# Batch 0's q and k loaded as f32 rows of all heads, turned on TensorE as f32, and a new order of the first steps

## The chip, the cores and the metric

The kernel runs on one core of a Trainium2 chip. The metric is the device time of one execution in microseconds (us); lower is better. TensorE (PE in the profile) multiplies matrices into PSUM; VectorE (DVE), ScalarE (ACT) and GpSimd (POOL) work on tiles; SyncE (SP) only issues transfers. Transfers are also issued by GpSimd, which alone can cast f32 to bf16 on the way, and by ScalarE. All of them run on the same 16 DMA engines.

## The reference

```
q, k, v: (8, 8, 576, 64) f32        # batch, heads, tokens, head dim
scores = q @ k^T / 8, kept where 0 <= row - col < 64, else -1e9
attn   = softmax(scores) @ v
x      = attn as (4608 tokens, 512)  # heads side by side
h      = x @ w_in                    # (4608, 2048)
out    = (h * cos(h)) @ w_out        # (4608, 512) f32
```

## The kernel before

**Tiling.** Attention runs by batch, by head pair p (4 pairs, two heads on 128 partitions) and by unit j (64 query rows that see 128 keys at most). A group is up to four units, one PSUM bank of scores. The feed-forward part runs by token tiles of 512 (mt 0 to 8); mt 0 is tokens 0 to 511 of batch 0 and is computed in two halves of 256 tokens. From mt 1 on, feed-forward matmuls (`first`, line 453, into `h_ps`; line 609, into `out_ps`) are laid out by a loop, and the attention steps of the next batch are put between them by a plan with times (`at`, `pump`). That part is the same in both kernels.

**The first stretch** is written out by hand: the string `FIRST` is a list of steps, each issued in that order; an engine runs its own instructions in that order. A step is a name and its arguments; the last letter is often the engine (a ScalarE, d VectorE, p GpSimd, s SyncE). The names:

- `Lq0.p`, `Lk0.p` load q, k of batch 0, one head pair: pair 0 as f32 on SyncE (`load_plain`, then `cq`, `ck` cast it), pairs 1 to 3 through GpSimd with a cast (`load_heads`), 128 runs of 2304 bytes. `Lq1`, `Lk1` are batch 1, `Lq2`, `Lk2` batch 2, `Lv0.c`, `Lv1.c` chunks of v (128 tokens by 8 heads, 1024 runs of 256 bytes), `Lwi.i`, `Lwo.i` quarters of w_in and w_out (512 runs of 2 KB each).
- `tq`, `tk` turn q, k of a pair of batch 0 on TensorE (18 transposes of 64x64 bf16 into a PSUM tile of the pool `ps_t`, which has three), `pq`, `pk` copy them out to `qT` (scaled) and `kT`. `Tq`, `Tk`, `Pq`, `Pk` do so for batch 1.
- For a group: `s` scores (line 293 puts the mask, line 309 adds the products), `m` the row maximum (line 319, VectorE), `e` the exponentials (line 336, ScalarE, four instructions), `i` the reciprocal of the sums (line 346), `n` the product with it (line 353, mostly GpSimd), `w` the turn of the weights (line 364), `c` their copy out to `wT`. `G...` are the same steps for groups of batch 1 and the last rows of batch 0.
- `z...`, `y...` copy v into the odd slots that lie across chunks; `v.a.g` is the product with v for two pairs and a half (line 403), `x.a.g` its copy to `xT`. `h.g.f` is the feed-forward product of half g and block f (line 417; needs both `x.0.g` and `x.1.g`), `S` its sine, `g` the gate; `o`, `oc` the second product (line 436) and its copy out. `io`, `mk`, `mc` make the masks, `ms` clears blocks for later batches.

Groups of batch 0 are, before, four units in a row of one pair: `s.p.g` is pair p, units 4g to 4g+3. `FILL` adds transposes and a matmul without use at two groups.

Of the kernel before, what the change touches and what calls it, by code (L numbers as in the profile page):

```python
# [10 lines left out]
def _safe_warn(msg, *a, **kw):  # L11
# [14 lines left out]
GF = 4  # L26
# [18 lines left out]
FILL = (6, 12)  # L45
# [5 lines left out]
    "io ms.0.d Lq0.0 Lk0.0 ms.1.d mk cq.d ms.2.d mc ck.a tq.0 Lq0.1 pq.0.d Lk0.1 tk.0 pk.0.a s.0.0.0 "  # L51
    "Lq0.2 tq.1 tk.1 m.0.0 pq.1.a ms.3.d s.0.1.1 Lk0.2 tq.2 pk.1.d s.1.0.2 Lq0.3 Lk0.3 tk.2 s.1.1.3 "
    "e.0.0 tq.3 m.0.1 Lq1.0 Lk1.0 Lq1.1 pq.2.d pk.2.d Lk1.1 tk.3 m.1.0 s.2.0.4 Lv0.0 Lv0.1 Tq.0 Lv0.2 "
    "pk.3.d m.2.0 e.0.1 pq.3.a i.0.0 e.1.0 Tk.0 s.3.0.0 Tq.1 e.2.0 Lv0.3 Lwi.0 Pq.0.d i.1.0 Lwi.1 m.3.0 "
    "m.1.1 i.2.0 Pk.0.a e.3.0 Lwi.2 Tk.1 n.1.0.p s.2.1.1 Pq.1.d Gs.10.2 m.2.1 Gs.9.4 n.0.0.p Pk.1.a "
    "n.2.0.p i.3.0 e.1.1 w.0.0 zA.0.d w.1.0 c.0.0.d Gs.12.0 w.2.0 n.3.0.p i.0.1 c.1.0.d zA.1.d c.2.0.d "
    "e.2.1 zB.0.s zB.1.s n.0.1.p i.1.1 w.3.0 v.0.0 c.3.0.d x.0.0.a s.3.1.3 Gm.10 v.1.0 m.3.1 i.2.1 "
    "Gs.11.2 Gm.9 Gm.12 n.1.1.p x.1.0.a e.3.1 ms.4.d w.0.1 w.1.1 c.1.1.a i.3.1 h.0.0.1 h.0.1.4 tb "
    "n.2.1.p c.0.1.d Lwi.3 w.2.1 h.0.2.0 n.3.1.p v.0.1 S.0.0 Gm.11 w.3.1 S.0.1 h.0.3.3 Lwo.0 S.0.2 "
    "c.2.1.d c.3.1.d v.1.1 zC.s g.0.0 S.0.3 h.0.4.2 ms.5.d x.0.1.a x.1.1.d h.0.5.1 g.0.1 h.1.0.4 g.0.2 "  # L60
    "g.0.3 S.0.4 ms.6.d h.0.6.0 h.1.1.3 S.0.5 S.1.0 Lq1.2 S.0.6 g.0.4 S.1.1 g.1.0 h.1.2.2 Lk1.2 ms.7.d "
    "Lq1.3 h.0.7.4 g.0.5 h.1.3.1 Lv1.0 Lwo.1 g.1.1 S.1.2 h.1.4.3 g.0.6 Lk1.3 S.0.7 h.1.5.0 g.1.2 h.1.6.2 "
    "Lwo.2 g.0.7 S.1.3 S.1.4 S.1.5 Lwo.3 h.1.7.4 Lv1.1 S.1.6 g.1.3 g.1.4 S.1.7 g.1.5 Lv1.2 g.1.6 tb2 "
    "Tk.2 Lv1.3 Pk.2.d Ge.10 Tq.2 Pq.2.d Tq.3 Ge.9 Ge.12 o.0.0.1 Pq.3.d Tk.3 o.1.0 Pk.3.d Lv0.4 Lq2.0 "
    "Ge.11 Gs.14.3 Gi.10 Gm.14 g.1.7 Lq2.1 Gs.13.0 Lq2.2 o.0.1.2 Gi.9 o.2.0 Ge.14 Gn.10.p Gm.13 Gc.10 "
    "Gi.12 Gs.8.3 o.1.1 Gs.16.4 Gm.8 o.3.0 Ge.13 o.2.1 Gs.15.0 Gi.11 oc.0.d Gn.9.p o.3.1 Gn.12.p o.0.2.3 "
    "Gi.14 Gm.15 Gs.17.1 oc.1.d Gc.9 Gn.11.p Gi.13 Gm.16 o.1.2 Ge.8 Ge.16 Ge.15 y.1.d Gn.14.p yA.p Gi.8 "
    "Gc.12 Gm.17 o.0.3.0 Gi.16 Gn.13.p yB.p Gc.11 Gn.8.p Lq2.3 Lq2.4 Lq2.5 o.2.2 Gn.16.d Gw.8 Gc.14 "
    "Gc.13 Lk2.0 Gp.8.d o.3.2 Gi.15 Gw.16 Lk2.1 Ge.17 Lk2.2 o.1.3 Gn.15.d V.0 Gp.16.d oc.2.a Gw.15 Gi.17 "
    "Lk2.3 o.2.3 V.1 Gp.15.d X.0.a Gn.17.d X.1.d V.2 V.3 X.2.a X.3.d Gc.17 o.3.3 oc.3.a Gs.18.4 Gm.18 "  # L70
    "Ge.18 Lk2.4 Gi.18 Gn.18.d Gc.18 Lk2.5 Lv1.4 "
# [4 lines left out]
def kernel(  # L76
# [28 lines left out]
    first_q = moe.tile([128, 2, d_model], F32, tag="out", name="qT", bufs=OUTS).rearrange("p a f -> p (a f)").bitcast(BF16)  # L105
    qtiles = [first_q[:, S * i:S * i + S] for i in range(PAIRS - 1)]
    qtiles.append(const.tile([128, S], BF16, name="qT3"))
    turned = const.tile([128, PAIRS, S], BF16, name="qT")
    qtiles += [turned[:, p] for p in range(PAIRS)]
    qsets = [const.tile([128, PAIRS, NU, 2, 64], BF16, name=f"qB{i}") for i in range(2)]  # L110
    qblocks = [qset[:, p] for qset in qsets for p in range(PAIRS)]
    vtiles = [const.tile([128, NU - 1, d_model], BF16, name=f"v{i}") for i in range(2)]
    w_in_sb = const.tile([128, PAIRS, d_ff], BF16, name="w_in")
    w_out_sb = const.tile([128, n_ff, d_model], BF16, name="w_out")
    w_in_v = moe_w_in.rearrange("(a p) f -> p a f", p=128)
    w_out_v = moe_w_out.rearrange("(a p) f -> p a f", p=128)
    ident = const.tile([128, 128], BF16, name="ident")
    mask = const.tile([128, 3, 128], F32, name="mask")
    mask16 = const.tile([128, 6, 128], BF16, name="mask16")
# [16 lines left out]
    def copy(engine, out, in_):  # L136
        {"a": nc.scalar.copy, "p": nc.gpsimd.tensor_copy}.get(engine, nc.vector.tensor_copy)(out, in_)  # L137
# [15 lines left out]
    def cast_masks():  # L153
        for lo, hi, of in ((0, 3, 0), (3, 5, 1), (5, 6, 1)):
            nc.scalar.copy(mask16[:, lo:hi], mask[:, of:of + hi - lo])


    def rows_tile(name):
        return ld.tile([128, NC * H * D], BF16, tag=name, name=name)

    def load_heads(name, b, p0=0, n=PAIRS):
        if (name, b) not in st:
            st[name, b] = rows_tile(name)[:, 0:PAIRS * RC * D].rearrange("p (a x) -> p a x", a=PAIRS)
        src = {"q": q, "k": k}[name][b, 2 * p0:2 * p0 + 2 * n]
        nc.gpsimd.dma_start(out=st[name, b][:, p0:p0 + n],
                            in_=src.rearrange("(a h) (p c) d -> (h p) a (c d)", h=2, c=RC))

    def load_plain(name):
        rows = moe.tile([128, 2, d_model], F32, tag="out", name="rows", bufs=OUTS).rearrange("p a f -> p (a f)")[:, 0:RC * D]
        st["rows", name] = rows  # L170
        nc.sync.dma_start(out=rows, in_={"q": q, "k": k}[name][0, 0:2].rearrange("h (p c) d -> (h p) (c d)", c=RC))

    def cast_plain(name, engine):
        if (name, 0) not in st:
            st[name, 0] = rows_tile(name)[:, 0:PAIRS * RC * D].rearrange("p (a x) -> p a x", a=PAIRS)
        copy(engine, st[name, 0][:, 0], st.pop(("rows", name)))
# [49 lines left out]
    def tr_q(b, p):  # L226
        st["tq", b, p] = transposed("q", b, p)

    def put_q(b, p, engine=None):
        of, to = in_order(st.pop(("tq", b, p)), qtiles[b * PAIRS + p], b)  # L230
        if b:
            copy(engine, to, of)
        elif engine == "a":
            nc.scalar.mul(to, of, scale)
        else:
            nc.vector.tensor_scalar(to, of, scale, None, ALU.mult)
# [31 lines left out]
    groups = [[(0, p, j) for j in range(GF * g, GF * g + GF)] for p in range(PAIRS) for g in range(TU // GF)]  # L268
# [13 lines left out]
    def g_scores(n, which):  # L282
        s_ps = bank((BANKS if n < n_listed else S_BANKS)[which], "s_ps")
        units = groups[n]
        if n == FILL[1]:
            nc.tensor.matmul(out=s_ps, lhsT=ident, rhs=mask16[:, 0:4].rearrange("p u c -> p (u c)"), start=True, stop=True,
                             skip_group_check=True)
        s_ps = s_ps[:, 0:len(units) * 128].rearrange("p (u c) -> p u c", c=128)
        if n < n_first:
            m0 = 2 if units[0][2] else 0  # L290
            for h in range(2):
                d = slice(64 * h, 64 * h + 64)
                nc.tensor.matmul(out=s_ps[d].rearrange("p u c -> p (u c)"), lhsT=ident[d, d],
                                 rhs=mask16[d, m0:m0 + len(units)].rearrange("p u c -> p (u c)"),
                                 start=True, stop=False, skip_group_check=True)
# [61 lines left out]
    def g_trans(n):  # L357
        w, u = st.pop(("w", n)), len(groups[n])
        if n in direct:
            st["tw", n] = t_ps = ps_t.tile([128, GF, 128], BF16, tag="t", name="tw_ps")  # L360
            for i in range(GF if n == FILL[0] else 0):
                nc.tensor.transpose(t_ps[:, i], ident, ident)
            for i in range(u):
                nc.tensor.transpose(t_ps[:, i], w[:, i], ident)  # L364
            return
        wT = att.tile([128, GF, 128], BF16, tag="wT", name="wT", bufs=20)
        nc.sync.dma_start(out=wT[:, 0:u], in_=w[:, 0:u].rearrange("p u c -> p (u c)"), transpose=True)
        st.update({("wT", unit): wT[:, i] for i, unit in enumerate(groups[n])})
# [172 lines left out]
    make_identity(nc, ident)  # L541
# [6 lines left out]
    def spread_first(lo, hi):  # L548
        return lambda i, engine: spread_v(0, i, engine, lo, hi)

    steps = {"Lq0": lambda p: load_heads("q", 0, p, 1) if p else load_plain("q"),
             "Lk0": lambda p: load_heads("k", 0, p, 1) if p else load_plain("k"),
             "cq": lambda engine: cast_plain("q", engine), "ck": lambda engine: cast_plain("k", engine),
             "Lq1": lambda p: load_heads("q", 1, p, 1), "Lk1": lambda p: load_heads("k", 1, p, 1),
# [4 lines left out]
             "tq": lambda p: tr_q(0, p), "tk": lambda p: tr_k(0, p), "Tq": lambda p: tr_q(1, p), "Tk": lambda p: tr_k(1, p),  # L559
             "pq": lambda p, engine: put_q(0, p, engine), "pk": lambda p, engine: put_k(0, p, engine),  # L560
# [4 lines left out]
             "s": lambda p, g, which: g_scores(2 * p + g, which), "m": lambda p, g: g_max(2 * p + g),  # L565
             "e": lambda p, g: g_exp(2 * p + g), "i": lambda p, g: g_inv(2 * p + g),
             "n": lambda p, g, engine: g_norm(2 * p + g, engine), "w": lambda p, g: g_trans(2 * p + g),
             "c": lambda p, g, engine: g_put(2 * p + g, engine), "v": values_half, "x": put_x_half,
# [80 lines left out]
```

## Time and profile before

| | |
|---|---|
| time, median of 3 runs | 308.87 us (308.71 to 309.77) |
| profiled execution: span from first to last instruction | 306.3 us |
| its own time beside the span | not given by the page; median less span is 2.6 us |
| busy: TensorE, VectorE, ScalarE, GpSimd | 97%, 75%, 76%, 63% |
| granted TensorE clock | 1.00 |
| first `h` matmul (line 417) | 21.18 us |
| first matmul of token tile 1 (line 453) | 57.17 us |
| moved by GpSimd's queue q0 | 100192 packets, 18.06 MB |
| moved by SyncE's queue q1 | 59568 packets, 23.38 MB |

The page follows one execution. Busy time counts overlapping instructions of an engine once, and matmuls are pipelined, so 97% is not the share of the peak. The chain of waits goes back from the last instruction through what released each step. In the tables of queues a packet is one descriptor, that is one run of bytes; the share is the sum of their times against the 16 engines' time and passes 100% where several are in flight on an engine.

### The profile page before, as it was taken

The numbers are of one execution on the slowest core, as the hardware profiler recorded it, in microseconds if no ns is written. First come the engines' busy times: TensorE is split into PE (matmuls) and PEld (weight loads), VectorE is DVE, ScalarE is ACT, GpSimd is POOL, SyncE is SP. The second block draws the span as 40 slices with busy tenths as digits, with TensorE's granted clock in tenths as the row PEclk, the third lists the DMA queues.
The fourth block names the chain that finished last, engine by engine and source line by source line (L and its number), as shares of the span: only waits on it lengthen the run. The fifth ranks groups of instructions, "written<-read, shape, count | busy, mean of one in ns | idle before, by whom it ended". The sixth has DMA issues, their size and how long they took to land.

```text
span 306.3 us, 7904 instructions
## 1 busy us (share of the span) xinstructions
PE 296.2 (97%) x2616; PEld 159.0 (52%) x2616; DVE 228.5 (75%) x908; ACT 234.3 (76%) x785; POOL 192.5 (63%) x228
## 2 busy tenths in 40 slices
PE   3889999999999999999999999999999999999996
PEld 2768844545555555445544555454545554454443
DVE  5999978599769976798579857986698668235801
ACT  5998799677997799779976997699879986116600
POOL 8998579995659669967998599959903930000000
PEclk9999999999999999999999999999999999999999
DMA  7999999999999995999999999999794643011011
GB/s 146 179 212 192 200 180 130 121 149 191 226 113 116 175 223 80 121 133 232 125 121 137 231 143 104 157 221 148 86 137 107 169 78 141 2 68 71 1 67 70
DMA packets 159945, 42.14 MB, mean 138 GB/s; under 512 B 148256, under 2 KB 155168, under 8 KB 159904
## 3 DMA queue, kind: packets, MB, share of 16 engines
q0 software_dynamic: 100192, 18.06, 80.1%
q1 hardware_dynamic: 59568, 23.38, 40.6%
q8 instruction: 20, 0.33, 0.4%
q14 instruction: 21, 0.17, 0.2%
q10 hardware_dynamic: 144, 0.20, 0.2%
HBM read 36.70 MB, written 9.44 MB: 151 GB/s over the span
## 4 chain that ended last, share of the span: by engine, by line
PE 90%; POOL 4%; DMA 2%; DVE 1%; ACT 1%; issue 1%; POOLq 0%; DVEq 0%; ACTq 0%
PE h_ps L453 35%; PE out_ps L609 35%; PE h_ps L417 5%; PE s_ps L303 4%; PE out_ps L436 4%; PE o_ps L384 3%; DMA k<-in_k_dram 2%; POOL w L353 2%; PE tq_ps L219 1%; POOL v L188 1%; PE out_ps L465 1%; PE s_ps L309 1%; PE tw_ps L364 1%; POOL w_in L204 1%; ACT e L336 1%
## 5 line engine op out<-in xcount | busy, mean ns | idle before, releaser
L609 PE MATMUL out_ps<-w_out,gT 128*128 128x512 bf16 x496 | 117.3, 379 | 0.0
L453 PE MATMUL h_ps<-xT,w_in 128*128 128x512 bf16 x512 | 115.3, 379 | 0.3
L595 ACT ACTIVATE sin<-h_ps 128x512 f32<-128x512 f32 x128 | 73.7, 598 | 32.7 <-PE h_ps L453 31.4
L598 DVE TENSOR_TENSOR gT<-h_ps,sin 128x512 bf16<-128x512 f32 x128 | 82.1, 685 | 21.9 <-ACT sin L595 21.2
L336 ACT ACTIVATE e<-s,negm 128x128 f32<-128x128 f32 (+1 forms) x256 | 97.1, 382 | 0.6 <-DVE negm L324 0.6
L353 POOL TENSOR_TENSOR w<-e,rden 128x512 bf16<-128x512 f32 (+1 forms) x74 | 70.0, 962 | 36.6 <-DVE rden L346 18.8
L453 PEld LDWEIGHTS <-w_in 128*128 128x128 bf16 x512 | 48.8, 98 | 54.7 <-issue 0.4
L609 PEld LDWEIGHTS <-gT 128*128 128x128 bf16 x496 | 45.9, 98 | 44.2
L324 DVE CUSTOM_DVE_ANT_0 s<-s_ps,mask 128x128 f32<-128x128 f32 (+1 forms) x256 | 56.4, 279 | 1.7 <-PE s_ps L309 0.9
L336 ACT ACTIVATION_READ_ACCUMULATOR e<-s,negm 128x1 f32 x256 | 48.3, 189 | 0.0
L182 POOL DMA_DIRECT2D q<-in_q_dram x36 | 28.3, 785 | 10.7 <-DMA q<-in_q_dram 4.0
L188 POOL DMA_DIRECT2D v<-in_v_dram x40 | 34.4, 878 | 0.3 <-issue 0.2
L182 POOL DMA_DIRECT2D k<-in_k_dram x36 | 28.2, 783 | 3.9 <-DMA k<-in_k_dram 1.2
L137 ACT COPY out_sb<-out_ps 128x512 f32<-128x512 f32 (+1 forms) x18 | 10.2, 566 | 24.5 <-PE out_ps L609 18.4
L346 DVE RECIPROCAL rden<-den 128x4 f32<-128x4 f32 (+1 forms) x79 | 13.1, 166 | 19.0 <-ACT e L336 18.6
L303 PEld LDWEIGHTS <-qB 128*128 128x128 bf16 x216 | 16.5, 98 | 14.2
L137 DVE CAST xT<-o_ps 128x512 bf16<-128x512 f32 x24 | 15.5, 677 | 10.1 <-PE o_ps L384 10.1
L137 DVE COPY out_sb<-out_ps 128x512 f32<-128x512 f32 x18 | 12.4, 690 | 13.2 <-PE out_ps L609 12.5
L324 DVE DVE_READ_ACCUMULATOR2_ANT negm<- 128x1 f32 x256 | 21.3, 83 | 0.0
L303 PE MATMUL s_ps<-kT,qB 128*128 128x128 bf16 (+1 forms) x216 | 21.2, 216 | 0.0
L137 POOL COPY v<-v 64x1536 bf16<-64x1536 bf16 (+3 forms) x12 | 18.8, 1570 | 0.3
L137 DVE COPY qB<-tq_ps 64x384 bf16<-64x384 bf16 (+1 forms) x40 | 15.6, 390 | 0.4
(70 smaller groups left out, 257.8 us busy)
## 6 DMA issues: line engine op xcount, KB each, us to landing
out_dram<-out_sb SPq DMA_DIRECT2D x16, 512.0 KB, 7.5
v<-in_v_dram POOLq DMA_DIRECT2D x32, 128.0 KB, 5.7
q<-in_q_dram POOLq DMA_DIRECT2D x36, 96.0 KB, 8.6
k<-in_k_dram POOLq DMA_DIRECT2D x36, 96.0 KB, 8.5
w_in<-in_moe_w_in_dram POOLq DMA_DIRECT2D x4, 512.0 KB, 8.7
w_out<-in_moe_w_out_dram POOLq DMA_DIRECT2D x4, 512.0 KB, 10.8
wT<-w SPq DMA_TRANSPOSE x68, 4.4
q<-in_q_dram POOLq DMA_DIRECT2D x7, 144.0 KB, 6.0
```

The costliest lines, as they stand in the source:

```text
L137: {"a": nc.scalar.copy, "p": nc.gpsimd.tensor_copy}.get(engine, nc.vector.tensor_copy)(out, in_)
L182: nc.gpsimd.dma_start(out=st[name, b][:, c].rearrange("p (h d) -> p h d", h=H), in_=src.rearrange("h p d -> p h d"))
L188: nc.gpsimd.dma_start(out=vt.rearrange("p (h d) -> p h d", h=H), in_=v[b, :, c * 128:c * 128 + n, :].rearrange("h p d -> p h d"))
L303: nc.tensor.matmul(out=s_ps[:, u, 0:64 * chunks].rearrange("p (a t) -> p a t", a=chunks), lhsT=qblocks[(b % 2) * PAIRS + p][:, j].rearrang ...
L324: nc.vector.tensor_tensor_reduce(out=s[:, u, c], in0=s_ps[:, u, c], in1=mask[:, 2 - j % 2 if j else 0, c], scale=-scale if b else -1.0, sc ...
L336: nc.scalar.activation(e[:, u, c], s[:, u, c], AF.Exp, bias=negm[:, u:u + 1], scale=1.0 if n < n_first else -1.0, accum_out=den[:, u:u + 1])
L353: (nc.gpsimd if engine == "p" else nc.vector).tensor_tensor(out=w[:, 0:u], in0=e[:, 0:u], op=ALU.mult, in1=rden[:, 0:u].unsqueeze(2).to_br ...
L417: nc.tensor.matmul(out=h_ps[:, half * e:half * e + half], lhsT=w_in_sb[:, ks, ff * 128:ff * 128 + 128], rhs=st["xT", 0][:, ks, half * g:ha ...
L453: nc.tensor.matmul(out=st["h", ff], lhsT=w_in_sb[:, ks, ff * 128:ff * 128 + 128], rhs=st["xT", mt][:, ks], start=start, stop=stop)
L595: nc.scalar.activation(sin, h_ps, AF.Sin, bias=math.pi / 2.0)
L598: nc.vector.tensor_tensor(out=gt[:, e], in0=h_ps, in1=sin, op=ALU.mult)
L609: nc.tensor.matmul(out=o_ps[e], lhsT=gT[ff // 2][:, ff % 2, ms * 128:ms * 128 + 128], rhs=w_out_sb[:, ff], start=ff == 0, stop=ff == n_ff - 1)
```

## The change

Batch 0's q and k are loaded by chunks of 128 tokens and all heads as f32 (`L.q.c`, `L.k.c`; 1024 runs of 256 bytes, the fifth chunk has 64 tokens), on SyncE, one of them on ScalarE. They are staged in the tile of w_out (the fifth chunk in a tile of its own). TensorE turns each chunk as f32, four transposes of 128x128 into one PSUM tile (`t.q.c`, `t.k.c`), and one copy per chunk casts it into place for all four pairs (`p.q.c`, `p.k.c`). Groups of batch 0 are now two pairs by two units, so that one group needs one chunk of q: `s.a.g` is pairs 2a and 2a+1, units 2g and 2g+1. FILL goes, and `FIRST` is a new order. In it GpSimd's queue begins with v and batch 1, and takes w_in by quarters 1, 2, 0, 3. On the engines, the first entries of the new order are:

```
SyncE:  k3 q3 q0 k1 q1 q2 k2, then q4 k4     (each 1024 runs, q4 and k4 512)
ScalarE: table load, k0, masks, p.q.0, e.0.0, p.q.2, e.1.0, e.1.1, e.0.1, Pk.1, e.1.3, e.0.3, e.0.2, x.1.0
GpSimd: ident, v0, iota, k of batch 1 (pairs 0, 1), v1, q of batch 1 (pairs 0, 1), w_in 1, v3, w_in 2,
        clear, w_in 0, n.0.0, v2, n.1.0, z, w_in 3, n.0.1, z, v4 of batch 1, n.1.3, w_out 1, ...
VectorE: masks, p.k.3, p.q.3, p.k.0, m.0.0, p.q.1, p.k.1, m.1.0, i.0.0, m.1.1, m.0.1, p.k.2, i.1.0, Pk.0, c.0.0,
        m.1.3, i.1.1, p.k.4, n.1.1, i.0.1, p.q.4, m.0.3, Pq.0, m.0.2, i.1.3, c.0.1, c.1.0, c.1.1, i.0.3, m.1.2, x.0.0
TensorE: t.k.3 t.q.3 t.q.0 t.k.0 s.0.0 t.q.1 s.1.0 t.k.1 t.q.2 s.1.1 s.0.1 t.k.2 Tk.0 w.0.0 s.1.3 t.k.4 Tk.1 s.0.2
        t.q.4 s.0.3 Tq.0 w.0.1 w.1.0 w.1.1 Gs.8 s.1.2 Gs.10 v.0.0 Gs.9 v.1.0 Tq.1 w.1.3 h.0.2 h.0.3 h.0.5 ...
```

```diff
-    first_q = moe.tile([128, 2, d_model], F32, tag="out", name="qT", bufs=OUTS).rearrange("p a f -> p (a f)").bitcast(BF16)
...
+    stage = w_out_sb.rearrange("p a f -> p (a f)").bitcast(F32).rearrange("p (c x) -> p c x", c=8)
...
+    ident32 = const.tile([128, 128], F32, name="ident32")
...
-    def load_plain(name):
-        rows = moe.tile([128, 2, d_model], F32, tag="out", name="rows", bufs=OUTS).rearrange("p a f -> p (a f)")[:, 0:RC * D]
-        st["rows", name] = rows
-        nc.sync.dma_start(out=rows, in_={"q": q, "k": k}[name][0, 0:2].rearrange("h (p c) d -> (h p) (c d)", c=RC))
...
+    def load_rows(name, c, queue):
+        (nc.scalar if queue == "a" else nc.sync).dma_start(
+            out=rows_of(name, c).rearrange("p (h d) -> p h d", h=H),
+            in_={"q": q, "k": k}[name][0, :, 128 * c:min(128 * c + 128, S)].rearrange("h p d -> p h d"))
+
+    def turn_rows(name, c):
+        of = rows_of(name, c)
+        n = of.shape[0]
+        st["t", name, c] = t_ps = ps_t.tile([128, PAIRS, n], F32, tag="t", name=f"t{name}_ps")
+        for p in range(PAIRS):
+            nc.tensor.transpose(t_ps[:, p], of[:, 128 * p:128 * p + 128], ident32[:n, :n])
+
+    def put_rows(name, c, engine):
+        t_ps = st.pop(("t", name, c))
+        to = (first_q if name == "q" else k_tile(0))[:, :, 128 * c:min(128 * c + 128, S)]
...
-    groups = [[(0, p, j) for j in range(GF * g, GF * g + GF)] for p in range(PAIRS) for g in range(TU // GF)]
+    groups = [[(0, p, j) for p in (p0, p0 + 1) for j in (j0, j0 + 1)] for p0 in (0, 2) for j0 in range(0, TU, 2)]
...
-        if n == FILL[1]:
-            nc.tensor.matmul(out=s_ps, lhsT=ident, rhs=mask16[:, 0:4].rearrange("p u c -> p (u c)"), start=True, stop=True,
-                             skip_group_check=True)
...
-            for i in range(GF if n == FILL[0] else 0):
-                nc.tensor.transpose(t_ps[:, i], ident, ident)
```

## The prediction

> **What bounds the kernel now.** I read four views: the chain of waits, the timeline of TensorE around the first feed-forward matmul, the transfer queues in short windows, the timelines of VectorE and GpSimd up to 22 us. Engines and lines of the chain first:
>
> ```profile
> PE 90%; POOL 4%; DMA 2%; DVE 1%; ACT 1%; issue 1%; POOLq 0%; DVEq 0%; ACTq 0%
> ```
>
> TensorE is 90% of it. The timeline shows from where (start, length, engine, line):
>
> ```profile
> 20.72 0.62 PE L364 MATMUL tw_ps<-ident,w 128*128 128x128 bf16 x8
> 21.18 1.93 PE L417 MATMUL h_ps<-xT,w_in 128*128 128x256 bf16 x16
> ...
> 57.17 2.76 PE L453 MATMUL h_ps<-xT,w_in 128*128 128x512 bf16 x12
> ```
>
> From 21.18, the first `h`, matmuls follow each other almost without a gap, to 57.17 (second token tile) and on to the end. So the time is the start of the first `h`, plus TensorE's work behind it, plus new stalls. Behind 57.17 the program is the same. What lies ahead of 21.18 is attention on batch 0, fed by transfers. The queues (packets, MB, share of 16 engines), in windows 43 to 46 us, 17 to 20 us, 7 to 11 us, 75 to 76 us (the last two lines):
>
> ```profile
> q0 software_dynamic: 3651, 0.46, 240.9%
> ```
> ```profile
> q0 software_dynamic: 608, 0.61, 122.7%
> ```
> ```profile
> q0 software_dynamic: 729, 0.75, 116.5%
> ```
> ```profile
> q1 hardware_dynamic: 154, 0.31, 89.6%
> q0 software_dynamic: 155, 0.02, 28.2%
> ```
>
> q0 is GpSimd's queue, q1 SyncE's. Per engine (divide by 16) a descriptor costs: a 256-byte run of v, 3651 in 3 us, 13 ns; a 2 KB run of w_in, 608 in 3 us, 79 ns; a 2304-byte run of q or k, some 648 (81 of the 729 are under 512 bytes) in 4 us, 99 ns. In the last window q0 has small v runs and q1 large stores: 155 against 154, one for one. A small descriptor that shares with a queue of large ones waits for a large one each time: 104 ns per pair instead of 13.
>
> **The change part by part.** *Loads of batch 0.* Out go two plain loads and six pair loads (128 runs of 2304 bytes each). In come eight loads of 128 rows by 8 heads, 1024 runs of 256 bytes, 64 per engine, and two halves. Seven of the full ones go through SyncE in the order k3 q3 q0 k1 q1 q2 k2, then q4 k4; k0 goes through ScalarE behind its table load (2.24). At the same time GpSimd's queue, which before issued all of q and k first, gets v0, both k pairs of batch 1, v1, both q pairs, w_in 1, v3, w_in 2, w_in 0, none with a wait ahead. Its issues (0.56 to 0.9 each) run ahead of its transfers, so it is never empty.
>
> Per engine: SyncE's data flows from 2.3 (as the plain loads do), GpSimd's from 3.9. By 3.9 SyncE has moved 122 descriptors. Then 70 (rest of q3, q0) + 64 (k0) + 64 (v0), 13 ns each: 2.6, so q0 and k0 land at 6.5. Then one for one: k of batch 1, 16 x (99 + 13) = 1.8, to 8.3; v1, 64 x 26 = 1.7, to 10.0 (k1 done); q of batch 1, to 11.8; w_in 1, 32 x (79 + 13) = 2.95, to 14.7, when SyncE's 128th lands, the end of q1; v3 to 16.4 (q2); w_in 2 to 19.4; w_in 0 to 22.3, SyncE's 256th: k2. If SyncE were not held, k2 would land at 6.5 + 256 x 0.013 = 9.9. I take 22.3, since the window shows that share to a percent; 9.9 and 24 (a slower plain descriptor) bound it.
>
> The Trainium skill, page "DMA: Bandwidth & Descriptors", section "Queues, rings and completion order", says that an engine drains a whole packet, typically 9 to 17 descriptors, from one ring before it turns to the next. By that rule small descriptors would go in bunches and k2 would land near the early bound; the 154 to 155 above speaks against it here.
>
> *Turning.* 144 transposes of 64x64 go (18 took 0.46 once warm, 3.7 in all), 40 of f32 come. None is in the trace; bounds are 0.10 each (four bf16 128x128 ones took 0.40) and four times that. I take 0.7 a chunk, nearer the bf16 row. TensorE waits for data then, so only k2's 0.7 is on the path (0.4 to 1.6).
>
> *From k2 to the first `h`.* TensorE runs in order: t.k.2 stands ahead of s.1.3, s.0.2, s.0.3, s.1.2 and w.0.0, all needed before the first `h`. p.k.2 stands in VectorE's queue ahead of i.1.0, which releases n.1.0, GpSimd's second product. VectorE, per operation start to start from its timeline: max 0.645 (two took 1.29), turned copy 0.65, wT copy 0.39, reciprocal 0.1, x copy 0.65, half copy 0.35, product 0.65. Landed 22.4, t.k.2 to 23.1, p.k.2 to 23.9. Then up to x.0.0: four max 2.6, Pk.0 and Pq.0 1.3, four wT copies 1.55, five reciprocals 0.5, p.k.4 and p.q.4 0.7, n.1.1 0.65, x.0.0 0.65: 7.95, to 31.8. One wait in it, 0.4, for t.q.4, s.0.3: 32.2. GpSimd's chain from i.1.0 at 24.0 is nearly as long: three products at 1.04, two v copies at 1.07, the issues of w_in 3 (0.8) and of batch 1's v 4 (0.7), 6.8 in all, to 30.8, then w.1.3. ScalarE's e.1.3, e.0.3, e.0.2, x.1.0 end at about 31.9. So the first `h` starts at 32.2, 11.0 later than 21.18.
>
> *TensorE's work behind it.* The same 128 `h`, 64 `o`, 72 transposes of batch 1; one group of wT turns (4) and six score matmuls move behind the first `h`: 0.25 + 0.2 = 0.45. FILL's filler (0.4 + 0.4) lay ahead of 21.18 in waiting time: nothing.
>
> *VectorE behind it.* After x.0.0 it owes Gm.8, Gm.9, Gm.10 (12 x 0.21), n.1.2 and Pq.1 (1.3): 3.8, before g.0.2, while TensorE's four `h` and three turns cover 4.2; banks come free a little late: 0.6, from 0 to 1.5.
>
> *Clock.* In the trace 18 transposes take 0.69 up to 9.7 us and 0.46 from 10.3. The Trainium skill, "TensorE: Matmul & The Clock Gate", Part 1, puts such a pair down to a clock that halves after an idle window of about 3.4 us and doubles after a busy one; by it the emptier start would add an estimate of up to 1.7 at the first `h`. I take nothing for it; the upper end holds a cold stretch.
>
> *Hidden edits.* The iota moves behind one v issue (0.9) and the masks with it, to about 5.5; the scores need them at 9. Staging lies in w_out's tile, so w_out's loads wait for the turns; the last, issued near 45, is needed past 55 and landed in 10.8 before: without that cover 1 to 3. The batch-0 casts (0.46, 0.67) go into the first wait.
>
> *Sum.* The page gives no separate time for the profiled execution; its span is 306.3, the median 308.87, and I keep the 2.6 between them. 308.87 + 11.0 + 0.45 + 0.6 = 320.9, say 321.
>
> **The rivals.** *B, the loads are not held.* SyncE's small descriptors go in bunches and k2 lands near 10. Then VectorE decides: q0, k0 at 6.5, t.q.0 and t.k.0 to 8.0, p.k.0 to 8.7, scores and first max to 10.2; behind that p.q.1, p.k.1, three max, a reciprocal and p.k.2, 4.0, then the 7.95 and the 0.4: x.0.0 ends at 22.6, 1.4 late: 308.87 + 1.4 + 0.45 = 310.7, or 313 with the slow turns. For it: both plain loads of the trace landed 2.9 to 3.2 after issue. Against: the one-for-one window. This is also the case that the Trainium skill's rule on packets (above) would make.
>
> *C, faster.* Scores of all heads start as soon as two chunks are there, and ScalarE's exponentials set the pace: seven groups at 1.40 (four of 0.35), p.q.2 0.65, Pk.1 0.67, x.1.0 0.6: 11.7 behind e.0.0. If e.0.0 starts at 7.3, against 8.18 before, the first `h` is at 19.0: 308.87 - 2.2 + 0.45 = 307.1. It decides only if q0 lands by 4.5 and k2 by 9, and if VectorE's list of 13 behind p.k.0 is shorter than its rows say.
>
> *D, no change.* Between B and C: e.0.0 at 9, `h` at 20.7, 308.8.
>
> **How the numbers follow.** About 0.5%, 1.5 us, is what a measurement of this kernel can tell from no change. The forecast has 0.70, with 317 to 325 as its own range (k2 from 18.5 to 24.5, turns, stall). B has 0.19, C 0.07, D 0.04. Slower 0.89, same 0.04, faster 0.07. The range reaches down to 310 to take in B, up to 325; it leaves out C, D and some 0.08 above.
>
> **What would show it.** In the profile after: in the windows from 7 to 20 us, q1 has about as many packets as q0 whenever q0 moves 1 KB packets, and q1 is not through before 20; TensorE's t.k.2 ends past 20; between p.k.2 and x.0.0 VectorE is busy without a break; the first `h` is near 32 and the second tile's first matmul near 69. The forecast is wrong if q1's seven loads have landed by 12, or if the first `h` starts before 24.

## The result, and the profile after

| | before | after |
|---|---|---|
| time, median of 4 runs | 309.32 us | 325.89 us (324.59 to 326.81) |
| ratio | | 1.0523, 95% interval 1.0477 to 1.0569 |
| span of the profiled execution | 306.3 | 323.8 (its time 325.61) |
| first `h` | 21.18 | 37.17 (forecast 32.2) |
| k2 landed | | 27.13 (forecast 22.3) |

The change costs 5.2%. The forecast, 321.0, had the direction and the mechanism; 325.89 lies just above its range (310 to 325). Some executions take over 1.5% longer than the fastest of the same kernel, in a slower state, and medians here and below leave them out (one each of e5, e7 and e8). The chain of waits by engine and by line, from the page:

```profile
PE 80%; DMA 7%; DVE 5%; ACT 4%; SPq 2%; issue 1%
PE h_ps L462 34%; PE out_ps L616 30%; DMA w_out<-in_k_dram 6%; PE s_ps L314 3%; ACT e L347 3%; PE o_ps L393 3%; PE h_ps L426 3%; SPq L176 2%; PE out_ps L445 2%; DMA wT<-w 2%; PE tq_ps L238 1%; DVE w L364 1%; PE out_ps L474 1%; DVE s L335 1%; PE s_ps L320 1%
```

TensorE carried 90% of the chain before. Now 6% of it, 18.85 us, is one transfer: k2, staged in w_out's tile, from its issue at 8.28 to its landing at 27.13; SyncE's issues ahead of it (L176) are on the chain too. TensorE's timeline (start, length, engine, line, what it waited for in brackets):

```profile
11.37 0.53 PE L320 MATMUL s_ps<-kT,qB 64*64 64x64 bf16 x8 [0.22 <-DVE kT L136]
17.86 1.09 PE L185 MATMUL tq_ps<-ident,w_out 128*128 128x128 f32 x4 [5.97 <-DMA w_out<-in_q_dram]
...
27.27 1.09 PE L185 MATMUL tk_ps<-ident,w_out 128*128 128x128 f32 x4 [3.33 <-DMA w_out<-in_k_dram]
...
37.17 3.00 PE L426 MATMUL h_ps<-xT,w_in 128*128 128x256 bf16 x26
...
74.88 2.76 PE L462 MATMUL h_ps<-xT,w_in 128*128 128x512 bf16 x11
```

TensorE waits 5.97 for q1 and 3.33 for k2. The first `h` is 16.0 later than before, the second tile's first matmul 17.7, the end 17.5: nearly all of the loss is in place when the first `h` starts.

The queues (packets, MB, share of 16 engines), in windows 5 to 6, 13 to 15, 17 to 18 and 20 to 24 us; q0 is GpSimd's, q1 SyncE's, q10 ScalarE's:

```profile
q0 software_dynamic: 481, 0.06, 95.1%
q10 hardware_dynamic: 397, 0.10, 60.6%
q1 hardware_dynamic: 89, 0.02, 15.1%
```
```profile
q0 software_dynamic: 307, 0.31, 91.3%
q1 hardware_dynamic: 310, 0.08, 29.8%
```
```profile
q0 software_dynamic: 412, 0.05, 80.1%
q1 hardware_dynamic: 412, 0.10, 79.5%
```
```profile
q0 software_dynamic: 627, 0.63, 91.9%
q1 hardware_dynamic: 633, 0.16, 30.1%
```

310 beside 307, 412 beside 412, 633 beside 627: one for one, whether GpSimd's run is a row of w_in (second and fourth window) or of v (third, the load v3). Divided by 16 engines, a pair of SyncE's 256 bytes and a run of w_in costs 2 us x 16 / 308 = 104 ns, a pair of two small ones 39 ns. The first window is different: while ScalarE's k0 and GpSimd's v0 flow, SyncE hardly moves. So it is again beside v1: from 10.2 to 11.2 us SyncE moved 104 packets and GpSimd 854.

SyncE's issues show the backlog from the other side (start, length):

```profile
1.25 1.52 SPq L176 DMA_DIRECT2D w_out<-in_q_dram  x2
2.82 0.91 SPq L176 DMA_DIRECT2D w_out<-in_k_dram  x1
3.77 4.47 SPq L176 DMA_DIRECT2D w_out<-in_q_dram  x2
8.28 5.71 SPq L176 DMA_DIRECT2D w_out<-in_k_dram  x1
```

The first four issues take 0.45 to 0.91 each; that of k2 takes 5.71.

### The profile page after: what moved, and what is told of

It reads as the page before. It is cut to its first block, busy times and chain, and to the rows that moved or that the text cites. A ratio compares the mean times of both kernels' runs of the same rounds, so it can differ in the third digit from the quotient of the medians.

```text
span 323.8 us, 7659 instructions
## 1 busy us (share of the span) xinstructions
PE 300.3 (93%) x2475; PEld 163.2 (50%) x2507; DVE 229.1 (71%) x907; ACT 232.2 (72%) x782; POOL 194.6 (60%) x224
## 4 chain that ended last, share of the span: by engine, by line
PE 80%; DMA 7%; DVE 5%; ACT 4%; SPq 2%; issue 1%
PE h_ps L462 34%; PE out_ps L616 30%; DMA w_out<-in_k_dram 6%; PE s_ps L314 3%; ACT e L347 3%; PE o_ps L393 3%; PE h_ps L426 3%; SPq L176 2%; PE out_ps L445 2%; DMA wT<-w 2%; PE tq_ps L238 1%; DVE w L364 1%; PE out_ps L474 1%; DVE s L335 1%; PE s_ps L320 1%
## 5 line engine op out<-in xcount | busy, mean ns | idle before, releaser
L616 PE MATMUL out_ps<-w_out,gT 128*128 128x512 bf16 x482 | 114.6, 379 | 0.8 <-issue 0.2
L364 POOL TENSOR_TENSOR w<-e,rden 128x512 bf16<-128x512 f32 (+1 forms) x70 | 66.5, 963 | 58.6 <-DVE rden L357 54.9
L136 ACT COPY out_sb<-out_ps 128x512 f32<-128x512 f32 (+1 forms) x18 | 10.2, 565 | 23.9 <-PE out_ps L616 18.4
L357 DVE RECIPROCAL rden<-den 128x4 f32<-128x4 f32 (+1 forms) x79 | 12.9, 165 | 17.7 <-ACT e L347 17.5
L136 DVE CAST xT<-o_ps 128x512 bf16<-128x512 f32 x25 | 16.3, 679 | 10.4 <-PE o_ps L393 10.4
L136 POOL COPY v<-v 64x2048 bf16<-64x2048 bf16 (+3 forms) x15 | 21.8, 1455 | 0.5
L136 DVE COPY out_sb<-out_ps 128x512 f32<-128x512 f32 x18 | 12.4, 689 | 13.1 <-PE out_ps L616 12.5
L314 PE MATMUL s_ps<-kT,qB 128*128 128x128 bf16 (+1 forms) x216 | 21.2, 216 | 0.1
```

Source lines behind the costliest of these rows:

```text
L314: nc.tensor.matmul(out=s_ps[:, u, 0:64 * chunks].rearrange("p (a t) -> p a t", a=chunks), lhsT=qblocks[(b % 2) * PAIRS + p][:, j].rearrang ...
L357: nc.vector.reciprocal(out=rden[:, 0:len(groups[n])], in_=den[:, 0:len(groups[n])])
L364: (nc.gpsimd if engine == "p" else nc.vector).tensor_tensor(out=w[:, 0:u], in0=e[:, 0:u], op=ALU.mult, in1=rden[:, 0:u].unsqueeze(2).to_br ...
L616: nc.tensor.matmul(out=o_ps[e], lhsT=gT[ff // 2][:, ff % 2, ms * 128:ms * 128 + 128], rhs=w_out_sb[:, ff], start=ff == 0, stop=ff == n_ff - 1)
```

## Experiments

The theory, H: SyncE's 256-byte descriptors are held by GpSimd's, and the last chunk that they bring sets the first `h`. The main rivals: SyncE's own pace (I), sharing by bytes (Y), and that the order and the f32 turns cost it, not the loads (N, T). Each kernel below is the changed kernel with one edit, e6 on with edits that build on each other. "Span less first h" shows how far the first `h` alone sets the time.

| kernel | k2 landed | first h | span | span less first h | median, ratio to before (95%) |
|---|---|---|---|---|---|
| before | | 21.18 | 306.3 | 285.1 | |
| after | 27.13 | 37.17 | 323.8 | 286.6 | 325.89, 1.0523 (1.0477 to 1.0569) |
| e1 big loads late | 14.90 | 32.47 | 319.7 | 287.2 | 321.17, 1.034 (1.0307 to 1.0373) |
| e2 w_in late | 18.77 | 33.26 | 319.0 | 285.7 | 320.76 (one run) |
| e3 k0 on SyncE | 27.67 | 39.03 | 325.1 | 286.1 | 326.92 (one run) |
| e4 long runs | 12.39 | 29.42 | 315.4 | 286.0 | 317.41, 1.0238 (1.0193 to 1.0284) |
| e9 long runs, k0 on SyncE | 13.50 | 25.37 | 311.5 | 286.1 | 312.93, 1.0106 (1.0075 to 1.0137) |
| e5 clears first | before 17.3 | 32.26 | 317.7 | 285.4 | 316.79, 1.0191 (1.0106 to 1.0276) |
| e6 chunks in order of need | 11.39 | 31.35 | 317.9 | 286.6 | 321.1, 1.0346 (1.0285 to 1.0407) |
| e7 and all ten early | 12.05 | 26.97 | 313.2 | 286.2 | 317.69, 1.0213 (1.0135 to 1.029) |
| e10 and v later | 9.89 | 25.68 | 311.5 | 285.8 | 314.17, 1.0155 (1.0127 to 1.0183) |
| e8 first half early | 11.92 | 33.59 | 319.3 | 285.7 | 321.07, 1.041 (1.0303 to 1.0516) |
| e11 e8 with e10's loads | 10.18 | 29.83 | 316.3 | 286.5 | 317.99, 1.0304 (1.0239 to 1.0369) |

Over thirteen kernels whose first `h` lies between 21.2 and 39.0 the last difference stays within 285.1 and 287.2. So what is to be explained is the first `h`. (e5, e6, e7, e8 and e11 spread by 2 to 4 us from run to run; the first `h` and the span are those of one traced execution, in e7 the fastest, 314.93.)

**e1, e2: take GpSimd's loads away from SyncE's.** e1 moves five issues behind the first product, e2 the three of w_in alone:

```diff
-... mc Lk1.0.2 Lv0.1 Lq1.0.2 L.q.0.s ... Lwi.1 L.k.1.s ... Lwi.2 ms.6.p Lwi.0 i.0.0 n.0.0.p s.1.1.2
+... mc Lv0.1 L.q.0.s ... L.k.1.s ... ms.6.p i.0.0 n.0.0.p Lk1.0.2 Lwi.0 Lq1.0.2 Lwi.1 Lwi.2 s.1.1.2
```

> GpSimd's five long-run loads (k pairs and q pairs of batch 1, w_in 0, 1, 2) are issued behind its first product n.0.0 instead of ahead of it; all else as in the changed kernel. Theory H (the loads of batch 0 are held: each 256-byte descriptor of SyncE waits for one of GpSimd's): only v stays beside SyncE, 64 small ones a load at 39 ns for a pair, 15.8 ns for one alone; from q0 at 7.6: 128 pairs 5.0, 128 alone 2.0, k2 lands at 14.6 (13.5 to 16) instead of 27.1, SyncE's long issues (3.5, 5.7) shrink below 2.5, the first h starts at 24.4 to 26.5 (GpSimd's five issues, 3.9, now stand between its products), time 312.5 to 315.5. Rival I (SyncE's own writing of 1024 descriptors is what is slow): issues and k2 stay as they are, k2 above 25, time above 322. Rival N (the new order and the f32 turns cost it, not the loads): k2 lands early, but the first h stays above 32.

> Only the three w_in loads go behind n.0.0; the pairs of batch 1 stay ahead. Theory H: from q0 at 7.6, k pairs 16 x 128 ns, v1 64 x 39, q pairs 16 x 128, v3 64 x 39, then 96 alone at 15.8: k2 at 18.2 (17 to 19.5), first h near 28.2, time 315.5 to 318. Rival I: k2 above 25. If instead bytes are what is shared, k2 lies near the middle between 14.6 and 27.1, above 20.

k2 landed at 14.90 (14.6 expected) and 18.77 (18.2): theory H, and rival I, SyncE's own pace, is out as the cause. In e1 the total fits better than its path: between 9 and 10 us v took the engines almost alone, and SyncE followed alone, not pair by pair.

```profile
q0 software_dynamic: 1181, 0.15, 233.9%
q1 hardware_dynamic: 25, 0.01, 4.6%
```

The first `h` moved far less than k2: 4.7 in e1, 3.9 in e2, where 10.7 to 12.8 and 9 were expected. The missing part is in TensorE's order and in new waits that the edits brought. In e1 TensorE came to t.k.2 at 18.03 only, 3.1 behind k2 (t.k.2, then Tk.0):

```profile
18.03 0.69 PE L185 MATMUL tk_ps<-ident,w_out 128*128 128x128 f32 x4
21.95 0.69 PE L235 MATMUL tk_ps<-ident,k 64*64 64x64 bf16 x18 [3.24 <-DMA k<-in_k_dram]
```

The k pairs of batch 1, now issued at 17.88, land at 21.91, and Tk.0 stands in TensorE's order ahead of everything that `h` needs. In e2 q1, at 15.75, was still held by v and the pairs, so that TensorE came to t.k.2 at 21.53 only, and behind it GpSimd's second product stood behind three issues of w_in (TensorE waited 2.46 for the products).

**e3: one queue or two.** k0 goes through SyncE, between q3 and q0.

```diff
-L.k.3.s t.k.3 L.k.0.a L.q.3.s t.q.3
+L.k.3.s t.k.3 L.q.3.s L.k.0.s t.q.3
```

> k0 goes through SyncE, behind q3 and ahead of q0, instead of through ScalarE. Theory F (SyncE's and ScalarE's descriptors stand in one line, in the order of their issues; in the changed kernel q0's waited while k0's flowed): q0, k0, k1, k2 land within 0.6 of before (8.6, 7.3, 11.7, 27.1), time within 1.5 us of the changed kernel. Rival S (two queues share side by side, so that ScalarE's brought k0 for little): k0 or q0 lands over 1 later, and k2 over 1 later, as SyncE now has 64 more to wait with.

k0 landed at 8.74, q0 at 11.49 and k1 at 17.84, 1.5, 2.9 and 6.2 later than in the changed kernel, k2 only 0.5 later, where rival S had over 1 (GpSimd's loads had ended by 26.4, so that the last of SyncE's ran alone); the time of the one run was 1 us longer. Theory F falls by the landings, though its time, within 1.5, held: ScalarE's queue is a second one that takes its own share, and a load put there is one that SyncE's need not wait with. Why SyncE's own q0 stood still meanwhile (89 packets from 5 to 6 us) stays open.

**e4, e9: the same bytes in an eighth of the descriptors.**

```diff
-            out=rows_of(name, c).rearrange("p (h d) -> p h d", h=H),
-            in_={"q": q, "k": k}[name][0, :, 128 * c:min(128 * c + 128, S)].rearrange("h p d -> p h d"))
+            out=rows_of(name, c),
+            in_={"q": q, "k": k}[name][0, 2 * (c % 4):2 * (c % 4) + 2].rearrange("h (p c) d -> (h p) (c d)", c=8)[0:128 if c < 4 else 64])
```

> The chunk loads of batch 0 fetch the same number of bytes in runs of 2 KB (other rows of q and k: the values of batch 0 are not the reference's), 8 descriptors an engine and load instead of 64; GpSimd's loads and all else stay. Theory H (one for one by descriptors): 64 descriptors in all, each at about 91 ns, 33 of them beside v0's: k2 lands at 8.6 to 10.5, the first h at 23 to 25, where VectorE's list sets it, time 310.5 to 313.5. Rival Y (the queues share by bytes): SyncE keeps half of some 195 GB/s, k2 above 18, time above 317. Rival N (the new order and the turns cost most of it): k2 early, first h above 30, time above 318.

k2 landed at 12.39 beside the same loads of GpSimd: it is the number of descriptors that is shared, not the bytes (rival Y put k2 past 18). It was later than the 10.5 expected, and the time, 317.41, is above theory H's range; it is as long as rival Y had it, but not with Y's late k2. What stands out is one load: ScalarE issued k0 at 4.20 instead of 1.62, when SyncE had issued seven, and it landed at 12.55. TensorE of e4:

```profile
12.69 1.09 PE L185 MATMUL tk_ps<-ident,w_out 128*128 128x128 f32 x4 [6.06 <-DMA w_out<-in_k_dram]
...
29.42 3.66 PE L426 MATMUL h_ps<-xT,w_in 128*128 128x256 bf16 x32
```

e9 is e4 with e3's edit.

> The long-run chunk loads of e4 (2 KB runs, other rows of q and k, so that the values of batch 0 are not the reference's), with k0 on SyncE behind q3 instead of last in line through ScalarE. This is the changed kernel with its loads cheap in descriptors and nothing else altered; what is left over the kernel before is the price of the f32 turns, the groups and the order. Theory H: k0 5.5, q0 7.1, q1 10.4, k2 13.3; from q1 on TensorE's and VectorE's order takes 14.3 (in e5_clears_first q1 landed at 12.6, p.k.2 ended at 18.8 with no wait for k2, and the list is 8.0), first h at 24 to 25.5, time 312 to 314.5: of 16.6 us lost, some 12 are the held loads and 4 the rest. Rival N: first h at 28 or later, time above 316: then the loads are half of it at most.

k0 landed at 5.32, q1 at 10.95, k2 at 13.50, and TensorE's timeline of e9 has:

```profile
25.37 2.89 PE L426 MATMUL h_ps<-xT,w_in 128*128 128x256 bf16 x25
```

312.93 is as expected. This is the cleanest split of the loss: with f32 turns, groups and order untouched and the loads cheap in descriptors, 3.4 us are left (312.93 less the 309.54 of before on that chip), and from 7.6 us on TensorE's timeline up to the first `h` has no wait for a transfer. Of 16.6 us, some 13 are the loads. The one other difference, k0 through SyncE, made the changed kernel no faster in e3. How the 3.4 divide among turns, groups and order was not separated.

**e5, e6, e7, e10: can the 256-byte loads be kept?** e5 lets GpSimd clear blocks first, e6 adds the order of need, e7 puts q4 and k4 ahead too, e10 also moves v 0 and 1 behind the clears. The head of e10's list:

```diff
+io L.k.0.s t.k.0 L.q.0.s t.q.0 L.k.1.s L.q.1.s mk p.k.0.d mc p.q.0.a s.0.0.0 L.q.2.s ms.6.p t.k.1 p.k.1.d L.k.2.s ms.7.p
+m.0.0 e.0.0 s.1.0.1 t.q.1 p.q.1.d L.k.3.s m.1.0 e.1.0 ms.3.p s.1.1.2 t.q.2 L.q.3.s p.q.2.a L.q.4.s L.k.4.s m.1.1 e.1.1
+ms.2.p s.0.1.3 ms.1.p ms.0.p Lv0.0 Lv0.1 Lk1.0.2 Lwi.0 i.0.0 n.0.0.p t.k.2 p.k.2.d m.0.1 e.0.1 t.k.3 p.k.3.d Lq1.0.2 ...
```

> As the changed kernel, but GpSimd first issues v 0, 1 and 3, then does its clears of qB (six of 1.06 us, some of which stood later, one on VectorE), and only then issues the k pairs, w_in 0, the q pairs, w_in 1 and 2, none of them behind a product. Theory H plus its rest (the loads held cost about 9 of the 16.0 us by which the first h came late, the order of the steps the other 7): k2 lands at 14.5 to 16, the k pairs by 17.5, so that Tk.0 waits for nothing; t.k.2 stands at 18 as TensorE comes to it only then, p.k.2 ends near 19.4, the list of 8.0 follows, first h at 26.5 to 28.5, time 315 to 317.5. Rival P (the loads alone cost it; as the prediction's rival B had it): first h below 24, time below 313. Rival G (GpSimd's chain of products is what is late): first h above 30.

> GpSimd's clears and loads much as in the run with the clears first, and the chunks come in the order in which the scores need them: k0 q0 k1 q1 q2 k2 k3 q3 q4 k4, all through SyncE, with their turns and copies moved alike (k3 and q3 no longer first). Theory O (the order of the chunks is the rest: the first scores waited for the third and fourth load): k0 at 4.2, q0 at 5.2, e.0.0 starts near 8.5 instead of 12.7, VectorE's list of 13.4 from p.k.0 at 5.5 with some 3 of waits, first h at 21.5 to 24, time 310 to 313. Rival T (f32 turns and VectorE's copies set it whatever comes first): first h as in the run with the clears first, above 26, time above 315.

The first `h` came 4 (e5) and 7 us (e6) past the upper ends that were expected, mostly for the same reason. TensorE of e5, then of e6:

```profile
24.01 0.66 PE L185 MATMUL tk_ps<-ident,rest 64*128 64x64 f32 x4 [4.62 <-DMA rest<-in_k_dram]
```
```profile
16.94 0.63 PE L184 MATMUL tk_ps<-ident,w_out 128*128 128x128 f32 x4 [3.51 <-DMA w_out<-in_k_dram]
18.90 1.08 PE L184 MATMUL tq_ps<-ident,w_out 128*128 128x128 f32 x4 [1.33 <-DMA w_out<-in_q_dram]
```

In e5 the half chunk k4, in e6 the chunks k3 and q3 were still in SyncE's queue when GpSimd's long runs began: k4, half a load, landed at 23.87. The first two or three chunks came as early as e6 hoped; the last one decides. Rival T's numbers came for e6, but not by its reason: these are waits for transfers.

> As the run with the chunks in the order of need, and now all ten chunk loads, the halves q4 and k4 too, stand on SyncE's queue before any of GpSimd's long-run loads flows: GpSimd does six clears behind v 0 and 1 and issues the k pairs of batch 1 only at about 10. Theory H with O (whatever chunk is left in the queue when the long runs begin is what the in-order steps then wait for; with none left the order of need pays): k4 lands by 13.5, no step waits for a chunk after that, p.q.3 ends near 16, VectorE's list of 6.7 with about 1 of waits follows, first h at 23.5 to 25.5, time 311.5 to 314. Rival T (f32 turns, a slow TensorE clock and the order itself set it): first h at 28 or later, time above 315.5.

> As e7_chunks_alone, with GpSimd's six clears ahead of v 0 and 1 too, so that SyncE's ten chunk loads have the engines to themselves until about 11. Theory H: 576 descriptors at 15.8 ns from 2.0 end by 11.5 to 12.5 (k4), q1 by 7.5, the first h at 23.5 to 25.5, time 311.5 to 314. Rival J (SyncE's queue stands still between its loads for a reason of its own, with nothing beside it): k4 above 15, first h above 26.

e7 missed its range: k4 was caught (20.02), and TensorE waited 1.24 for it in the traced execution. That one took 314.93; the two others of the median took 317.69 and 318.74, and what they waited for was not traced. e10 gets all ten loads ahead, with the first `h` at 25.68 and 314.17, both just above the expected 25.5 and 314; k4 came at 15.05, as rival J had it and later than theory H's 12.5, but no step waited for it. Of 16.6 us lost, 4.6 are left, by moving steps alone. SyncE's issues in e10, with nothing beside them:

```profile
4.80 2.33 SPq L176 DMA_DIRECT2D w_out<-in_k_dram  x2
7.17 1.15 SPq L176 DMA_DIRECT2D w_out<-in_q_dram  x1
```

Issues of 1.15 instead of 5.71: the long ones came from the backlog and were not its cause. And SyncE alone has a pace of its own, below.

**e8, e11: the first half's steps ahead of the second's**, in e7's and e10's loads:

```diff
-Tk.0 Pk.0.d zA.0.p w.0.0 c.0.0.d s.1.3.4 m.1.3 Lwi.3 i.1.1 t.k.4 p.k.4.d n.1.1.d Tk.1 ... v.0.0 Lwo.1 n.0.3.p Lv1.1 x.0.0.d
+w.0.0 c.0.0.d Tk.0 Pk.0.d zA.0.p i.1.1 n.1.1.d i.0.1 n.0.1.p zA.1.p Tk.1 Pk.1.a w.1.0 c.1.0.d w.1.1 c.1.1.d
+s.1.3.4 m.1.3 Lwi.3 w.0.1 c.0.1.d s.0.3.1 v.0.0 x.0.0.d v.1.0 x.1.0.a e.1.3 m.0.3 e.0.3 ... t.k.4 p.k.4.d t.q.4 p.q.4.d ...
```

> As e7_chunks_alone, and the steps that only the second half of the rows needs (the halves' turns and copies, the fourth group's maxima, the turned q of batch 1) move behind the first half's values and x copies in the written order. Theory V1 (VectorE's list up to x.0.0 is what is left): x.0.0 about 4 earlier than in e7_chunks_alone, first h at 20 to 22.5, time 309 to 312. Rival V2 (the work is only moved: the second half's h or the first gates wait for it): first h earlier by 2 or more, but the time within 1.5 of e7_chunks_alone.

> The transfers of e10_clears_v with the written order of e8_half_early: what only the second half of the rows needs stands behind the first half's values. In e8 one chunk load that was left in the queue (q3, landed at 19) hid what this order does. Theory V1 (VectorE's list ahead of x.0.0 is what is left): x.0.0 ends at 20 to 22, first h at 21.5 to 24, time 309.5 to 312. Rival V2 (moved, not saved: the second half's h, the first gates or w_in's second part, landing at 23, wait instead): first h earlier than e10's 25.7, but the time within 1.5 of e10's 314.2.

Both are slower than the kernels that they came from, and both theories missed. In e8 q3 was caught behind the long runs (TensorE waited 5.30 for it, until 19.26). In e7, with the same chunk loads in the same order, q3 was issued at the same time (9.94, 9.91 in e8) and landed at 15.68; what made it late in e8 is open. In e11 x.0.0 ended at 23.5, 1.9 earlier than in e10, but the moved steps still stood ahead of the first `h` on TensorE, some of them waiting for VectorE, and the first `h` came at 29.83, 4.2 later. No kernel tried here beats the one before.

## Where the forecast held, and the step that was mis-sized

**What held.** The frame: time follows the first `h`, with little behind it (285.1 before, 286.6 after; 0.45 + 0.6 was forecast, 1.5 came, and the other kernels spread over more than that difference). The place: t.k.2 waits for k2, SyncE's last load that counts. The mechanism: held one for one, beside w_in and v3; beside v0 and v1 SyncE did worse than that, and for this the forecast had nothing. From k2 on, the steps came as written: p.k.2 ended 1.9 behind the landing (1.5 forecast), and VectorE's list from there to the end of x.0.0 took 8.06 (7.95 and a wait of 0.4 forecast, and there is one of 0.41):

```profile
28.39 0.69 DVE L136 CAST kT<-tk_ps 128x512 bf16<-128x512 f32 x1 [3.72 <-PE tk_ps L185]
29.00 0.17 DVE L357 RECIPROCAL rden<-den 128x4 f32<-128x4 f32 x1
...
30.55 0.69 DVE L330 TENSOR_REDUCE negm<-s_ps 128x4 f32<-128x512 f32 x1 [0.41 <-PE s_ps L320]
...
36.38 0.68 DVE L136 CAST xT<-o_ps 128x512 bf16<-128x512 f32 x1
```

**The step that was mis-sized is k2's landing, forecast for 22.3 and measured at 27.13, and its largest term is the price of a shared pair.** The sum added the prices that the two descriptors have alone: 13 + 13 beside v, 13 + 79 beside w_in. The measured pairs cost 39 and 104 ns. The window of before that was quoted already said 104 for a pair; the sum then used 92. For the third kind, 13 + 99 beside q and k, it was about right: 69 packets of GpSimd and 70 of SyncE went from 12 to 12.5 us, 115 ns a pair. (The 128 ns of e2's expectation is no pair's price: between 8 and 10 us v1 had begun to flow, and SyncE moved 457 packets beside 317.)

The 4.8 us divide as follows. By its packets q0 is through at 7.6, not 6.5 (SyncE stood still beside k0 and v0): 1.1. The 96 pairs with w_in cost 12 ns more each, the 64 with v3 13 more: 2.0. Counted over all engines, the 7 x 1024 packets up to k2 had gone by about 25.6, but k2 landed 1.5 later; the sum took the last packet for the landing: 1.5. Whether one engine lagged or the landing itself took so long was not separated. The remaining 0.2 is not a term but a balance: v1, for which the sum has 64 pairs, went almost alone, and SyncE in turn went almost alone from 7.5 to 8.2 (604 packets beside 43). The first `h` was 5.0 later than forecast, of which k2 is 4.8; the time was 4.9 above 321.0. The upper bound of 24 for k2 was thus too low as well. With 27.13 in place of 22.3 and nothing else altered, the sum gives 325.7.

**The turns** took 1.09 a chunk for 0.7, within the bounds given: +0.4. Where TensorE had been busy they took 0.66 (e5, at 17.32), and 18 transposes beside them 0.47, so 0.7 was the price at the faster clock. **The clock** at the first `h`: 18 transposes took 0.69 at 28.28 and 0.47 at 30.90, six us ahead of it, so taking nothing for it was right. By the Trainium skill, "TensorE: Matmul & The Clock Gate", Part 1, an emptier start could have cost an estimated 1.7 there at most. This trace shows no such cost at the first `h` itself. Another run does: the first 32 `h` matmuls took 4.46 in e11 and 3.66 in e4 and e7, 0.8 more.

**Rival B** (loads not held) had 0.19 at 310.7, or 313 with the slow turns. Its condition did not occur. That e9, where the loads are cheap, took 312.93 fits its sum, but not its path: k2 landed at 13.50 there, not near 10. For B's bunches, the traffic of the second window above (13 to 15 us, in 40 slices of 50 ns) is the test, since equal counts alone would also come from bunches of equal length:

```profile
GB/s 248 138 284 100 294 97 287 125 282 131 215 192 179 205 146 246 143 246 164 225 184 225 148 261 92 317 82 302 102 302 108 276 133 236 169 179 220 148 241 143
```

It swings up and down from slice to slice, 100 ns for a full swing, which is the 104 of one pair: one large and one small descriptor take turns. Bunches of nine would swing once in an estimated 0.9 us (9 x 104 ns). The rule on packets in the Trainium skill, "DMA: Bandwidth & Descriptors", section "Queues, rings and completion order", that an engine drains a whole packet of some 9 to 17 descriptors from one ring before it switches, is the one from which the prediction drew B. This trace does not agree with it.

## What to carry to other kernels

Price a load by its descriptors and by what the other queues hold at that time: here a queue of short runs beside one of long runs went at the long run's pace (104 ns for each), and the price of a pair is to be read from a window in which both flow, not added up from windows of each alone. Splitting a load into 256-byte runs for the sake of an early start paid in no kernel here, and it cost least where nothing with long runs was issued before its last descriptor was nearly through: in e10 issuing those later, and the chunks in the order of need, won back 12 us without touching any arithmetic. When a wait is moved, look for the next transfer in the same in-order list: four times here (e5 to e8) it was a following chunk that stopped TensorE.

## What was not expected of the hardware

SyncE alone does not keep its first pace: in e10 the chunk loads landed at 6.28, 7.48, 8.68, 9.89, 11.09 and 12.30, 1.20 apart, some 850 packets per us, where 1022 had gone in 3 to 4 us. Three times a queue with issued descriptors stood nearly still: SyncE's from 5 to 6 us and from 10.2 to 11.2 us in the changed kernel, and from 9 to 10 in e1 (25 packets beside 1181 of v). Each time a load of v was flowing, but beside v3, from 17 to 18 us, the two went one for one. What stops a queue and what starts it again was not tried.
